# Attention with decay and a two-layer FFN on one core: reciprocals keyed earlier, two decay copies on ACT, buffers of the turned pairs relaid

## The chip, the cores and the metric

The kernel runs on 1 core of one Trainium2 chip. Times are device microseconds (us) of the whole program. A core has TensorE (PE, with its weight loads shown apart as PEld), VectorE (DVE), ScalarE (ACT), GpSimd (POOL) and SyncE (SP), each with a queue of its own that it works off in order. Matrix products go from SBUF into PSUM banks; DMAs are issued by SP, POOL or ACT.

## The reference

```python
def _attn_ref(q, k, v, f):                     # B, H, S, D = 8, 8, 576, 64
    scores = (1.0 / np.sqrt(D)) * np.matmul(q, k.transpose(0, 1, 3, 2))
    cum = np.cumsum(np.log(np.clip(f, 0.0001, 1.0)), axis=-1)
    decay = cum[:, :, :, None] - cum[:, :, None, :]
    scores = np.where(causal, -1000000000.0, scores + decay)   # causal: above the diagonal
    scores = scores - np.max(scores, axis=-1, keepdims=True)
    attn = np.exp(scores)
    attn = attn / (np.sum(attn, axis=-1, keepdims=True) + 1e-09)
    return np.matmul(attn, v)

x = attn_out.transpose(0, 2, 1, 3).reshape(B * S, H * D)       # 4608 x 512
h = x @ w_in                                                   # 512 -> 2048
g = np.maximum(h, 0.0) + alpha * np.minimum(h, 0.0)
return g @ w_out                                               # 2048 -> 512
```

All data are fp32.

## The kernel before

**Pairs.** The attention works on 32 pairs of heads, n = 4 b + p (batch b, pair p). `load_n` brings in what a pair needs, `attention` makes it up. For each pair: raw Q and K are loaded (L474, L475); from pair 4 on they are split into a high part on ACT (L537) and a low part on POOL (L538), and a score is three products; `Z` is the decay term of the four query tiles, with the causal mask added, and `Zt` that of the last 64 rows. DVE adds scores and decay and takes the row minimum (L744, L620), ACT takes the exponential and its row sum (L579), and the exponentials must then be transposed so that P·V can be multiplied.

**Two ways to transpose.** Pairs 0 to 9 transpose on PE, through PSUM. Pairs 10 to 31 (`NX = (10, 32)`) are "turned": the exponentials of a pair go into one buffer `bE`, DVE transposes it in 32 x 32 blocks into a buffer `bm` (L754), and sixteen DMAs of 96 KB move the blocks to their partitions in a buffer `bTT` (L764), which P·V reads. Of these sixteen, those with j % 8 in (2, 4, 6) are issued by POOL, the other ten by SP. There is one `bE`, two `bm` and one `bTT`: `bTT` is `wf[:, 0:3072]`, which is given to its ring in `o_cq` (L956), and `bE` and both `bm` are cut out of `big`, which `swap` (L963) gives to their rings when the P·V of pair 9 is done. The rings are `rE`, `rM` and `rTT`. Raw Q and K have a ring `rqk` of two buffers up to pair 10; from pair 11 on they use `rqk1`, whose one buffer also comes with `swap`.

**The decay of the turned pairs.** From pair NZ = 10 on, `Z` and `Zt` are made by DVE transposes of stored rows (L483, L485). Then, for each head, two copies (L501, L502) and four additions of the mask (L504) on POOL, and one addition for `Zt` (L529).

**Quotients.** From pair 6 on the row sums of two pairs are handled together: at the odd pair, `quotients` adds the epsilon on ACT (L670), takes the reciprocal on DVE (L671), transposes it on PE (L673), copies it on ACT (L674), stores it to DRAM from SP (L679), and `fetch` reads it back, spread over partitions, in three DMAs from SP for each of the two pairs (L686). The outputs of P·V, which ACT copies out of PSUM (L831), are multiplied with them (L844, for turned pairs on POOL) and split into high and low parts (L846, L848) for the FFN.

**FFN.** `ffn1` of a batch can start when its four pairs are done: 16 column blocks of 12 products each, the result evacuated by ACT and DVE (L925, L928, L930) and stored to DRAM (L932). `ffn2` follows after all of the attention, in tiles of seven products (Strassen's scheme in Winograd's form), every one as three products of high and low parts.

**What sets the order.** Nothing is ordered by hand. Every piece of work is an `op` with an engine, an estimated cost, a key, the ops it depends on and the buffers it takes. `Plan.run` is a list scheduler: again and again it takes, over all engines, the op that can start first by its estimates (the engine free, the inputs ready, a buffer free in each ring), and among those of one engine that can start at the same time the one with the smallest key. This fixes the order in each engine's queue before the kernel runs. Keys of a pair are built from `k0 = NS * n` with `NS = 10`, so 10 is one pair's distance. The moves of a pair have `k0 + 8`, `quotients` has `k0 + 11`, the loads have `kl = k0 - 16`, the decay `kc = k0 - 7`. On the chip an engine whose next instruction has to wait holds up all that are queued behind it.

Of the kernel before, what the change touches and what calls it, by code (L numbers as in the profile page):

```python
# [8 lines left out]
F32 = mybir.dt.float32  # L9
# [30 lines left out]
HURRY = 25  # L40
LAG = 1000
VK, TK = 0.65, 5
CONV0, CONV = 30, 2.2
# [160 lines left out]
def attention_moe(  # L204
# [21 lines left out]
    dram = ctx.enter_context(tc.tile_pool(name="dram", bufs=1, space=bass.MemoryType.DRAM))  # L226
    c8 = dram.tile([B * H, S], F32, name="c8")

    hd = dram.tile([NW, 2, 128, NT], F32, name="hd")
# [34 lines left out]
    qkt = [sp.tile([128, QW + S], F32, name=f"rqk{i}") for i in range(2)]  # L264
    rqk, rqk1 = Ring(Store(qkt)), Ring(Store([]))
    rZ = Ring(Store([(sp.tile([128, 2, ZW], F32, name=f"Z{i}"), sp.tile([128, S], F32, name=f"Zt{i}")) for i in range(2)]))
# [15 lines left out]
    cl = wf[0 : B * H, 0:S]  # L282
    G0 = 2 * NX[0]
    GN = B * H - G0
# [48 lines left out]
    def c_po(n):  # L333
        return 60 + 2.3 * n
# [48 lines left out]
    for i, (a0, a1) in enumerate(PC):  # L383
# [6 lines left out]
              -100, [o_sc[i]], [bcu, bft]) for i, (a0, a1) in enumerate(PC)]  # L390
    o_c8 = op("SP", 400, lambda: sy.dma_start(c8, ft()), -49, o_8, [bft], kb=147)
    o_id = op("POOL", 600, lambda: make_identity(nc, ident), -98)

# [67 lines left out]
    def load_n(n, held):  # L461
# [3 lines left out]
        kl, kc, bh = NS * n - 16, NS * n - 7, b * H + 2 * p  # L465
        bqk, bZ = Buf(rqk1 if n > NX[0] else rqk), Buf(rZ)
        q_, k_ = (lambda: bqk.t[:, 0:QW]), (lambda: bqk.t[:, QW : QW + S])
# [19 lines left out]
        for h in range(2):  # L487
            if spread:
                got = [zz]
            elif first:  # L490
                bz_ = Buf(rH)
                up = op("PE", 4 * c_mm(512), lambda h=h, bz_=bz_: mm(bz_.t, row()[:, h], ft()[:, 0:512], True, True), -60 + h, o_8 + [o_row], [bft, brow, bz_])
                got = [op("ACT", c_act(512), lambda h=h, bz_=bz_: ac.activation(Z()[:, h, 0:512], bz_.t, AF.Copy), -60, [up], [bz_, bZ])]
            else:
                got = [op("SP", 400, lambda h=h: sy.dma_start(Z()[:, h, 0:512], c8[bh + h : bh + h + 1, 0:512].broadcast_to([128, 512])),
                          kl + 1, [o_c8], [bZ], kb=256)]
            if n >= NX[0]:
                zp = lambda a, b, s, h=h: Z()[:, h, a:b].rearrange("p (k s c) -> p k s c", s=s, c=32)
                zd, zc, zb = (lambda zp=zp: zp(0, 512, 4)), (lambda zp=zp: zp(512, 896, 3)), (lambda zp=zp: zp(896, 1152, 2))
                za, tk = (lambda zp=zp: zp(1152, 1280, 1)), (lambda: tri.rearrange("p (k s c) -> p k s c", s=1, c=32))  # L500
                ms = [op("POOL", c_po(256) / 2, lambda zc=zc, zd=zd: po.tensor_copy(zc()[:, :, 0:2], zd()[:, :, 0:2]), kc + 0.1, got, [bZ]),  # L501
                      op("POOL", c_po(128) / 2, lambda zb=zb, zd=zd: po.tensor_copy(zb()[:, :, 0:1], zd()[:, :, 0:1]), kc + 0.2, got, [bZ])]  # L502
                for to, i in ((zc, 2), (zb, 1), (za, 0), (zd, 3)):
                    ms.append(op("POOL", c_po(128), lambda to=to, i=i, zd=zd: po.tensor_tensor(  # L504
                        to()[:, :, -1:], zd()[:, :, i : i + 1], tk(), ALU.add), kc + 0.1, got + [o_mask], [bZ]))
                rz.append(ms)
                continue
# [19 lines left out]
        else:  # L527
            tz = [op("SP", 400, lambda h=h: sy.dma_start(Zt()[64 * h : 64 * h + 64], c8[bh + h : bh + h + 1].broadcast_to([64, S])), kl + 1, [o_c8], [bZ], kb=147) for h in range(2)]
        rt = op("POOL", 260, lambda: po.tensor_tensor(Zt()[:, 512:576], Zt()[:, 512:576], tri2, ALU.add), kc + 0.3, tz + [o_mask], [bZ])  # L529
# [15 lines left out]
    def attention(n):  # L545
# [175 lines left out]
        def tile(h, i, st, bS, s, c0):  # L721
# [28 lines left out]
            if turned:  # L750
# [7 lines left out]
                if (h, i) == (1, 1):  # L758
                    e3.append(op("DVE", c_tr(768), lambda: turn(2, 288, 384), k0 + TK + 4, [be[g][m][1] for g in range(2) for m in (0, 1)], [bE, bm]))
                    got = []  # L760
                    for j in range(16):
                        a, k = j // 4, j % 4
                        q_, e_ = ((sy, "SP"), (po, "POOL"))[j % 8 in (2, 4, 6)]
                        got.append(op(e_, 600, lambda a=a, k=k, q_=q_: q_.dma_start(  # L764
# [119 lines left out]
        else:  # L884
            if mate:
                waiting.pop()
            quotients(k0 + 11 - hurry)
        later_x.append(rest)
# [66 lines left out]
    o_qc = [op("SP", 400, lambda a=a, c=c: sy.dma_start(c[32 * a : 32 * a + 32], c[0:32]), kc_ + 2, o_tc, kb=128) for a in range(1, 4) for c in (cq, cq2)]  # L955
    o_cq = op("-", 0, lambda: rTT.store.items.append(wf[:, 0:3072]) or rTT.store.free.append((plan.t, 0)), 0, o_tc + o_qc)  # L956

    def sides(h):
        for c, s0 in ((cq, 0), (cq2, 16)):
            po.tensor_copy(ct[64 * h : 64 * h + 64, s0 : s0 + c.shape[1], NX[0] :], c[64 * h : 64 * h + 64, :, h:GN:2])  # L960

    o_ct = [op("POOL", c_po(S) + 60, lambda h=h: sides(h), kc_ + 3, [o_cq]) for h in range(2)]
    def swap():  # L963
        for st, t in [(rE.store, big[:, 0:EW]), (rM.store, big[:, EW : EW + 3072]), (rM.store, big[:, EW + 3072 :]), (rqk1.store, qkt[0])]:
            st.free.append((plan.t, len(st.items)))
            st.items.append(t)
# [302 lines left out]
```

## Time and profile before

| | |
|---|---|
| median of 3 runs | 1046.42 us (1045.65 to 1049.57) |
| the profiled execution: time, span | 1045.14 us, 1043.3 us |
| granted TensorE clock, mean | 0.995 |
| PE busy | 1028.2 us, 99% of the span |
| DVE, ACT, POOL busy | 802.0, 631.2, 403.8 us |
| POOL, DMA issue of moves (L764) | 66.4 us in 132 |
| POOL, the copies L501 and L502 | 17.4 and 11.6 us, 44 of each |

The span goes from the first to the last instruction of the profiled execution; its time is 1.8 us longer. A group of the profile is told by its line in the kernel, its engine, its operation and "out<-in" by the program's names, with buffer numbers left out. "Idle before, releaser" is the time for which the engine stood still ahead of such instructions, and what ended it. SPq and POOLq are the DMA queues' own instructions, that is the issuing of DMAs.

### The profile page before, as it was taken

The page shows a single profiled execution, that of the slowest core. Times are in us where ns is not written, and L with a number is a line of the kernel's source. Part 1 is how long each engine was busy: PE and PEld are TensorE (multiplying, and loading weights), DVE is VectorE, ACT ScalarE, POOL GpSimd, SP SyncE. Part 2 cuts the span into 40 slices and gives each one's busy share as a digit, 9 for nine tenths or more (in the row PEclk, how much of TensorE's full clock was granted, in tenths as well). Part 3 has the DMA queues.
Part 4 walks back from the last instruction along what each step waited for, and adds up shares of the span by engine and source line. Part 5 has one row for each costly group of instructions (what it writes and reads, how often), then busy time and mean ns, then how long its engine had stood idle before and what let it go on. Part 6 is the DMA issues. An engine that isn't in the chain of part 4 may idle for free.

```text
span 1043.3 us, 22505 instructions
## 1 busy us (share of the span) xinstructions
PE 1028.2 (99%) x7994; PEld 899.7 (86%) x7994; DVE 802.0 (77%) x1702; ACT 631.2 (61%) x1462; POOL 403.8 (39%) x719
## 2 busy tenths in 40 slices
PE   9999999998999999999999999999999999999998
PEld 5888888787887787887888888899999999999998
DVE  5786885886776776767742987599898888989994
ACT  6779896675666666656552665655464545546551
POOL 6487674878887888886641000000000000000000
PEclk9999999998999999999999999999999999999999
DMA  5876754676888778886776666463434335344411
GB/s 173 236 224 209 231 171 131 195 218 180 254 236 224 233 225 229 245 242 183 213 207 194 213 222 203 166 201 121 140 123 140 122 122 161 117 129 139 124 62 41
DMA packets 125230, 187.74 MB, mean 180 GB/s; under 512 B 20967, under 2 KB 70622, under 8 KB 125118
## 3 DMA queue, kind: packets, MB, share of 16 engines
q1 hardware_dynamic: 120606, 173.13, 54.6%
q0 software_dynamic: 4224, 12.98, 4.8%
q8 instruction: 63, 1.03, 0.4%
q14 instruction: 49, 0.40, 0.1%
q10 hardware_dynamic: 288, 0.20, 0.1%
HBM read 102.80 MB, written 48.52 MB: 145 GB/s over the span
## 4 chain that ended last, share of the span: by engine, by line
PE 88%; POOL 4%; DMA 3%; DVE 2%; SPq 1%; issue 1%; ACT 1%; DVEq 0%; ACTq 0%; POOLq 0%
PE bank L362 84%; PE bank L592 2%; DMA rqk<-in_qk_dram 2%; SPq L764 1%; POOL Z L504 1%; PE bank L422 1%; POOL Ql L538 1%; POOL Kl L538 0%; DMA rd<-R 0%; PE bank L632 0%; DMA hd<-hs 0%; DVE big L744 0%; PE bank L456 0%; POOL xs L844 0%; POOL Z L510 0%
## 5 line engine op out<-in xcount | busy, mean ns | idle before, releaser
L362 PE MATMUL bank<-xx,wi 128*128 128x512 f32 x1728 | 418.2, 395 | 0.7 <-ACT eT L633 0.7
L362 PEld LDWEIGHTS bank<-xx,wi 128*128 128x128 f32 x1728 | 317.6, 188 | 74.1 <-issue 3.8
L579 ACT ACTIVATE big<-big,st 128x384 f32<-128x384 f32 (+4 forms) x268 | 156.1, 585 | 16.6 <-DVE st L744 15.1
L930 DVE SCALAR_TENSOR_TENSOR hs<-bank,sa,hs 128x512 f32<-128x512 f32 x96 | 71.7, 747 | 93.3 <-ACT hs L928 93.0
L362 PE MATMUL bank<-wot,xx 128*128 128x256 f32 x1008 | 123.9, 283 | 0.0
L362 PE MATMUL bank<-wi,xx 128*128 128x256 f32 x1008 | 123.9, 283 | 0.0
L362 PEld LDWEIGHTS bank<-wot,xx 128*128 128x128 f32 x1008 | 122.3, 192 | 0.0
L362 PEld LDWEIGHTS bank<-wi,xx 128*128 128x128 f32 x1008 | 122.3, 192 | 0.0
L744 DVE CUSTOM_DVE_ANT_0 big<-bank,Z 128x384 f32<-128x384 f32 (+3 forms) x211 | 92.9, 485 | 31.0 <-PE bank L362 22.9
L928 ACT ACTIVATE hs<-bank,ab 128x512 f32<-128x512 f32 x96 | 65.9, 686 | 82.5 <-PE bank L362 76.2
L754 DVE STREAM_TRANSPOSE big<-big 128x1152 f32<-128x1152 f32 (+1 forms) x66 | 79.3, 1221 | 13.6 <-ACT big L579 11.3
L764 POOL DMA_DIRECT2D wr<-big x132 | 66.4, 508 | 44.1 <-PE bank L632 24.7
L362 PE MATMUL bank<-wr,vr 128*64 128x128 f32 (+1 forms) x1232 | 68.3, 266 | 6.0 <-DMA wr<-big 4.2
L362 PEld LDWEIGHTS bank<-wr,vr 128*64 128x64 f32 x1232 | 60.1, 141 | 13.7 <-issue 6.9
L504 POOL TENSOR_TENSOR Z<-Z,tri 128x128 f32<-128x128 f32 x176 | 70.7, 428 | 0.0
L1153 ACT ACTIVATE xx<-gx 128x1024 fp32r<-128x1024 f32 x48 | 50.8, 1058 | 30.7 <-PE bank L362 15.1
L848 POOL TENSOR_TENSOR xx<-xs,xx 128x256 fp32r<-128x256 f32 x64 | 48.1, 764 | 49.4 <-ACT xx L846 49.0
L1156 DVE TENSOR_TENSOR xx<-gx,xx 128x1024 fp32r<-128x1024 f32 x48 | 58.5, 1218 | 7.9 <-ACT xx L1153 7.9
L362 PE MATMUL bank<-wi,gh 128*128 128x256 f32 x504 | 62.4, 283 | 0.0
L362 PE MATMUL bank<-wot,gh 128*128 128x256 f32 x504 | 62.4, 283 | 0.0
L362 PEld LDWEIGHTS bank<-wot,gh 128*128 128x128 f32 x504 | 61.4, 192 | 0.1
L362 PEld LDWEIGHTS bank<-wi,gh 128*128 128x128 f32 x504 | 61.3, 192 | 0.0
(157 smaller groups left out, 1749.4 us busy)
## 6 DMA issues: line engine op xcount, KB each, us to landing
hd<-hs SPq DMA_DIRECT2D x144, 256.0 KB
wx<-hd SPq DMA_DIRECT2D x47, 512.0 KB
wr<-big SPq DMA_DIRECT2D x220, 96.0 KB
rqk<-in_qk_dram SPq DMA_DIRECT2D x28, 512.0 KB
hr<-hd SPq DMA_DIRECT2D x25, 512.0 KB
wr<-big POOLq DMA_DIRECT2D x132, 96.0 KB, 3.7
vr<-in_vv_dram SPq DMA_DIRECT2D x32, 320.0 KB
wr<-in_w_in_dram SPq DMA_DIRECT2D x16, 512.0 KB
```

What stands on the lines that cost most here:

```text
L362: pe.matmul(o, lhsT, rhs, start=start, stop=stop)
L504: ms.append(op("POOL", c_po(128), lambda to=to, i=i, zd=zd: po.tensor_tensor(to()[:, :, -1:], zd()[:, :, i : i + 1], tk(), ALU.add), kc + ...
L579: ex = op("ACT", c_exp(w), lambda: ac.activation(at(bt.t), at(bt.t), AF.Exp, bias=lo()[:, col : col + 1], scale=-1.0, accum_out=su()[:, co ...
L592: pe.transpose(t[:, c : c + 128], src[:, 128 * j : 128 * j + 128], ident)
L744: ve.tensor_tensor_reduce(out=o if turned else blk(o), in0=blk(bS.t[:, c0 : c0 + w]), in1=in1(), scale=-0.125, scalar=3.0e38, op0=ALU.add, ...
L754: ve.transpose(part(bm.t), part(bE.t))
L764: got.append(op(e_, 600, lambda a=a, k=k, q_=q_: q_.dma_start(bTT.t[32 * k : 32 * k + 32, 768 * a : 768 * a + 768], bm.t[32 * a : 32 * a + ...
L848: xl = op("POOL", c_po(256), lambda r=r, t0=t0: po.tensor_tensor(bx.t[:, 1, t0 : t0 + 256], bxs[r].t[:, 0:256], bx.t[:, 0, t0 : t0 + 256]. ...
L928: cp = op("ACT", c_act(512), lambda bh=bh, bs=bs, fc=fc: ac.activation(bs.t, bh.t, AF.Relu, scale=ab[:, fc : fc + 1]), -1000, [last, o_sg] ...
L930: cp = op("DVE", c_dve(512), lambda bh=bh, bs=bs, fc=fc: ve.scalar_tensor_tensor(bs.t, bh.t, sa[:, fc : fc + 1], bs.t, ALU.mult, ALU.add), ...
L1153: his.append(op("ACT", c_acs(128 * GW * (j1 - j0)), lambda j0=j0, j1=j1, src=src, o_=o_: ac.activation(o_(0, j0, j1), src(), AF.Copy), key ...
L1156: rdy.append(op("DVE", c_dve(128 * GW * (j1 - j0)), lambda j0=j0, j1=j1, src=src, o_=o_: ve.tensor_tensor(o_(1, j0, j1), src(), o_(0, j0, ...
```

## The change

Four things are changed.

1. The key of `quotients` is lowered by 20 for turned pairs.
2. The two copies of the decay of a turned pair's head (L501, L502) are made by ACT instead of POOL, with the same keys and a cost estimate for ACT.
3. Buffers: `rqk1` is gone, so all raw Q and K share the ring `rqk` with its two buffers. `wf[:, 0:3072]` goes to `rM` (transposed blocks), and the last part of `big` goes to `rTT` (moved blocks). There are still one `bE`, two `bm` and one `bTT`.
4. A second copy of the decay rows in DRAM, `c8p`, whose columns are in the order of the turned pairs, is written by five DMAs from SP once `c8` is there. The loads of `Z` and `Zt` would read it for turned pairs below NZ; with `NX[0]` and NZ both 10 there is none. `PJ` names the three residues that were written out before, `G0` and `sides` name NZ where they named `NX[0]`, with the same values.

```diff
--- before.py
+++ after.py
@@ -39,6 +39,7 @@
 WC = 4
 HURRY = 25
 LAG = 1000
+PJ = (2, 4, 6)
 VK, TK = 0.65, 5
 CONV0, CONV = 30, 2.2
 NW = NF // 2
@@ -225,6 +226,7 @@
 
     dram = ctx.enter_context(tc.tile_pool(name="dram", bufs=1, space=bass.MemoryType.DRAM))
     c8 = dram.tile([B * H, S], F32, name="c8")
+    c8p = dram.tile([B * H, S], F32, name="c8p")
 
     hd = dram.tile([NW, 2, 128, NT], F32, name="hd")
     xt = dram.tile([NP, 128, 512], F32, name="xt")
@@ -262,7 +264,7 @@
 
     rQ = Ring(Store([split_set(i) for i in range(2)]))
     qkt = [sp.tile([128, QW + S], F32, name=f"rqk{i}") for i in range(2)]
-    rqk, rqk1 = Ring(Store(qkt)), Ring(Store([]))
+    rqk = Ring(Store(qkt))
     rZ = Ring(Store([(sp.tile([128, 2, ZW], F32, name=f"Z{i}"), sp.tile([128, S], F32, name=f"Zt{i}")) for i in range(2)]))
     vrt = sp.tile([128, 10, 2, D], F32, name="vr")
     rvr = Ring(Store([vrt[:, 5 * i : 5 * i + 5] for i in range(2)]))
@@ -280,7 +282,7 @@
     wf = wr.bitcast(F32)
     res = Ring(Store(cuts_of(1152, 2, 256) + [wf[:, 2560 + 256 * i : 2816 + 256 * i] for i in range(2)]))
     cl = wf[0 : B * H, 0:S]
-    G0 = 2 * NX[0]
+    G0 = 2 * NZ
     GN = B * H - G0
     cq = wf[:, 3072 : 3072 + 16 * GN].rearrange("p (s g) -> p s g", g=GN)
     rT4 = ring(sp, 2, [128, 128], F32, "eT4_")
@@ -389,6 +391,9 @@
     o_8 = [op("DVE", 150 + (a1 - a0) / 1.92, lambda a0=a0, a1=a1: ve.tensor_scalar_mul(ft()[:, a0:a1], cu()[:, a0:a1], -8.0),
               -100, [o_sc[i]], [bcu, bft]) for i, (a0, a1) in enumerate(PC)]
     o_c8 = op("SP", 400, lambda: sy.dma_start(c8, ft()), -49, o_8, [bft], kb=147)
+    o_c8p = [op("SP", 400, lambda k=k: sy.dma_start(c8p[:, 128 * k : 128 * k + 128].rearrange("p (s c) -> p s c", c=32),
+                                                    c8[:, 0:512].rearrange("p (s k c) -> p s k c", k=4, c=32)[:, :, k]), 6, [o_c8], kb=60) for k in range(4)]
+    o_c8p.append(op("SP", 400, lambda: sy.dma_start(c8p[:, 512:S], c8[:, 512:S]), 6, [o_c8], kb=16))
     o_id = op("POOL", 600, lambda: make_identity(nc, ident), -98)
 
     def make_mask():
@@ -463,7 +468,7 @@
         b, p = divmod(n, NP)
         first = n == 0
         kl, kc, bh = NS * n - 16, NS * n - 7, b * H + 2 * p
-        bqk, bZ = Buf(rqk1 if n > NX[0] else rqk), Buf(rZ)
+        bqk, bZ = Buf(rqk), Buf(rZ)
         q_, k_ = (lambda: bqk.t[:, 0:QW]), (lambda: bqk.t[:, QW : QW + S])
         kq = -99 if first else -59 if n == 1 else kl
         dq = [] if first else [o_scan]
@@ -492,14 +497,15 @@
                 up = op("PE", 4 * c_mm(512), lambda h=h, bz_=bz_: mm(bz_.t, row()[:, h], ft()[:, 0:512], True, True), -60 + h, o_8 + [o_row], [bft, brow, bz_])
                 got = [op("ACT", c_act(512), lambda h=h, bz_=bz_: ac.activation(Z()[:, h, 0:512], bz_.t, AF.Copy), -60, [up], [bz_, bZ])]
             else:
-                got = [op("SP", 400, lambda h=h: sy.dma_start(Z()[:, h, 0:512], c8[bh + h : bh + h + 1, 0:512].broadcast_to([128, 512])),
-                          kl + 1, [o_c8], [bZ], kb=256)]
+                c8_, o_ = (c8p, o_c8p) if n >= NX[0] else (c8, [o_c8])
+                got = [op("SP", 400, lambda h=h, c8_=c8_: sy.dma_start(Z()[:, h, 0:512], c8_[bh + h : bh + h + 1, 0:512].broadcast_to([128, 512])),
+                          kl + 1, o_, [bZ], kb=256)]
             if n >= NX[0]:
                 zp = lambda a, b, s, h=h: Z()[:, h, a:b].rearrange("p (k s c) -> p k s c", s=s, c=32)
                 zd, zc, zb = (lambda zp=zp: zp(0, 512, 4)), (lambda zp=zp: zp(512, 896, 3)), (lambda zp=zp: zp(896, 1152, 2))
                 za, tk = (lambda zp=zp: zp(1152, 1280, 1)), (lambda: tri.rearrange("p (k s c) -> p k s c", s=1, c=32))
-                ms = [op("POOL", c_po(256) / 2, lambda zc=zc, zd=zd: po.tensor_copy(zc()[:, :, 0:2], zd()[:, :, 0:2]), kc + 0.1, got, [bZ]),
-                      op("POOL", c_po(128) / 2, lambda zb=zb, zd=zd: po.tensor_copy(zb()[:, :, 0:1], zd()[:, :, 0:1]), kc + 0.2, got, [bZ])]
+                ms = [op("ACT", c_acs(256), lambda zc=zc, zd=zd: ac.activation(zc()[:, :, 0:2], zd()[:, :, 0:2], AF.Copy), kc + 0.1, got, [bZ]),
+                      op("ACT", c_acs(128), lambda zb=zb, zd=zd: ac.activation(zb()[:, :, 0:1], zd()[:, :, 0:1], AF.Copy), kc + 0.2, got, [bZ])]
                 for to, i in ((zc, 2), (zb, 1), (za, 0), (zd, 3)):
                     ms.append(op("POOL", c_po(128), lambda to=to, i=i, zd=zd: po.tensor_tensor(
                         to()[:, :, -1:], zd()[:, :, i : i + 1], tk(), ALU.add), kc + 0.1, got + [o_mask], [bZ]))
@@ -525,7 +531,7 @@
             tz = [op("ACT", c_act(a1 - a0), lambda b_=b_, a0=a0, a1=a1: ac.activation(Zt()[:, a0:a1], b_.t[:, 0 : a1 - a0], AF.Copy), -58, [up], [b_, bZ])
                   for b_, (a0, a1) in zip(bz2, cut)]
         else:
-            tz = [op("SP", 400, lambda h=h: sy.dma_start(Zt()[64 * h : 64 * h + 64], c8[bh + h : bh + h + 1].broadcast_to([64, S])), kl + 1, [o_c8], [bZ], kb=147) for h in range(2)]
+            tz = [op("SP", 400, lambda h=h, c8_=c8_: sy.dma_start(Zt()[64 * h : 64 * h + 64], c8_[bh + h : bh + h + 1].broadcast_to([64, S])), kl + 1, o_, [bZ], kb=147) for h in range(2)]
         rt = op("POOL", 260, lambda: po.tensor_tensor(Zt()[:, 512:576], Zt()[:, 512:576], tri2, ALU.add), kc + 0.3, tz + [o_mask], [bZ])
         if n < NN:
             held += [bqk]
@@ -760,7 +766,7 @@
                     got = []
                     for j in range(16):
                         a, k = j // 4, j % 4
-                        q_, e_ = ((sy, "SP"), (po, "POOL"))[j % 8 in (2, 4, 6)]
+                        q_, e_ = ((sy, "SP"), (po, "POOL"))[j % 8 in PJ]
                         got.append(op(e_, 600, lambda a=a, k=k, q_=q_: q_.dma_start(
                             bTT.t[32 * k : 32 * k + 32, 768 * a : 768 * a + 768], bm.t[32 * a : 32 * a + 32, 768 * k : 768 * k + 768]), k0 + 8 + j / 100, list(e3), [bm, bTT], kb=96))
                     e3[:] = [op("-", LAG, lambda: None, k0 + 8, got)]
@@ -884,7 +890,7 @@
         else:
             if mate:
                 waiting.pop()
-            quotients(k0 + 11 - hurry)
+            quotients(k0 + 11 - hurry - 20 * turned)
         later_x.append(rest)
         if n < NE - 1 or n == B * NP - 1:
             for f_ in later_x:
@@ -953,15 +959,15 @@
 
         o_tc.append(op("DVE", 340 + c_tr(S), spread_rows, kc_ + 1, o_cl + quick_ops + o_tc))
     o_qc = [op("SP", 400, lambda a=a, c=c: sy.dma_start(c[32 * a : 32 * a + 32], c[0:32]), kc_ + 2, o_tc, kb=128) for a in range(1, 4) for c in (cq, cq2)]
-    o_cq = op("-", 0, lambda: rTT.store.items.append(wf[:, 0:3072]) or rTT.store.free.append((plan.t, 0)), 0, o_tc + o_qc)
+    o_cq = op("-", 0, lambda: rM.store.free.append((plan.t, len(rM.store.items))) or rM.store.items.append(wf[:, 0:3072]), 0, o_tc + o_qc)
 
     def sides(h):
         for c, s0 in ((cq, 0), (cq2, 16)):
-            po.tensor_copy(ct[64 * h : 64 * h + 64, s0 : s0 + c.shape[1], NX[0] :], c[64 * h : 64 * h + 64, :, h:GN:2])
+            po.tensor_copy(ct[64 * h : 64 * h + 64, s0 : s0 + c.shape[1], NZ:], c[64 * h : 64 * h + 64, :, h:GN:2])
 
     o_ct = [op("POOL", c_po(S) + 60, lambda h=h: sides(h), kc_ + 3, [o_cq]) for h in range(2)]
     def swap():
-        for st, t in [(rE.store, big[:, 0:EW]), (rM.store, big[:, EW : EW + 3072]), (rM.store, big[:, EW + 3072 :]), (rqk1.store, qkt[0])]:
+        for st, t in [(rE.store, big[:, 0:EW]), (rM.store, big[:, EW : EW + 3072]), (rTT.store, big[:, EW + 3072 :])]:
             st.free.append((plan.t, len(st.items)))
             st.items.append(t)
 
```

## The prediction

> **What bounds the kernel now.** The page first: how busy the busiest engine is over the span.
>
> ```profile
> span 1043.3 us, 22505 instructions
> PE 1028.2 (99%) x7994; PEld 899.7 (86%) x7994; DVE 802.0 (77%) x1702; ACT 631.2 (61%) x1462; POOL 403.8 (39%) x719
> ```
>
> TensorE (PE) is idle for 1043.3 - 1028.2 = 15.1 us. The change adds and removes no matmul, so, slow clock apart, 15 us is about all that it can give. The view by stretches says where those 15 us lie. Columns: length, then busy us of PE, PEld, DVE, ACT, POOL, the granted clock, DMA share, GB/s. The turned pairs, which the change is about, lie between 180 and 560 us.
>
> ```profile
> 0.00:80.00 80.00, 76.71 (x645) 57.60 (x646) 57.84 (x175) 57.92 (x168) 52.01 (x98) 0.98 0.72 212
> 80.00:180.00 100.00, 100.00 (x837) 82.01 (x836) 71.20 (x158) 82.19 (x217) 61.46 (x85) 1.00 0.61 186
> 180.00:560.00 380.00, 371.80 (x2978) 300.70 (x2977) 269.21 (x641) 236.74 (x651) 286.43 (x533) 0.99 0.76 219
> 560.00:1043.30 483.30, 479.70 (x3540) 459.40 (x3538) 403.75 (x729) 254.39 (x429) 3.93 (x5) 1.00 0.45 142
> 241.00:248.00 7.00, 5.56 (x61) 5.27 (x61) 2.64 (x2) 1.78 (x5) 3.83 (x10) 0.51 0.47 144
> ```
>
> PE idles 3.3 us in the start, nothing from 80 to 180, 380 - 371.8 = 8.2 us among the turned pairs, and 3.6 us at the end, where only outputs are left. The change can reach the 8.2 us. The waits of PE between 160 and 560 us name them (total, times, longest):
>
> ```profile
> PE bank L362 <- DMA wr<-big: 4.2, 2, 3.6
> PE bank L362 <- DVE st L620: 1.4, 2, 0.7
> PE bank L362 <- ACT xs L831: 0.9, 1, 0.9
> PE bank L362 <- ACT eT L633: 0.7, 1, 0.7
> PE bank L673 <- DVE st L744: 0.4, 1, 0.4
> PE bank L362 <- DMA hd<-hs: 0.4, 1, 0.4
> ```
>
> One wait of 3.6 us is almost half of it. The timeline of PE shows what it really cost: the P·V products of one pair at full clock, and those after the wait, with the first instruction behind each.
>
> ```profile
> 228.00 1.75 PE L362 MATMUL bank<-wr,vr 128*64 128x128 f32 x28
> ...
> 230.91 0.33 PE L362 MATMUL bank<-Kh,Qh 64*128 64x128 f32 x2
> ...
> 242.44 3.26 PE L362 MATMUL bank<-wr,vr 128*64 128x128 f32 x28 [3.65 <-DMA wr<-big]
> ...
> 247.97 0.30 PE L632 MATMUL bank<-ident,big 128*64 128x128 f32 x1
> ```
>
> At full clock the products take 230.9 - 228.0 = 2.9 us; after the wait, at a clock of 0.51, 248.0 - 242.4 = 5.5 us. So this place costs 3.65 + 2.6 = 6.3 us, and the turned pairs hold 8.2 + 2.6 = 10.8 us in all. **That is the ceiling, 1.0%.** The bound for what can be told from no change is 0.5%, or 5.2 us.
>
> **Second raw Q, K buffer.** From pair 11 on all raw loads shared one buffer, so a load had to wait until the low parts of the pair before had been formed (SPq L474 <- POOL Kl). ACT runs in order and stands at the cast of Q until the load lands:
>
> ```profile
> SPq L474 <- POOL Kl L538: 5.7, 5, 2.5
> ```
>
> ```profile
> 332.53 0.74 ACT L537 ACTIVATE Qh<-rqk 128x640 fp32r<-128x640 f32 x1 [4.64 <-DMA rqk<-in_qk_dram]
> 333.18 0.25 ACT L633 ACTIVATE eT<-bank 64x128 f32<-64x128 f32 x1
> ...
> 396.81 0.74 ACT L537 ACTIVATE Qh<-rqk 128x640 fp32r<-128x640 f32 x1 [6.91 <-DMA rqk<-in_qk_dram]
> ...
> 399.98 0.37 ACT L831 ACTIVATE xs<-bank 128x256 f32<-128x256 f32 x1
> ```
>
> Behind the casts stand exactly the two ACT steps that PE waits for, L633 (0.7 us) and L831 (0.9 us). With two buffers the load is issued a pair earlier and both waits go: -1.6. What follows the second, the waits on DVE at L673 (0.4) and half of L620's (0.7), is ACT's lateness passed on: another -1.1. I take **-2.7**; bounds 0 (another step fills the same queue) and -3.8 (all six rows but the first: 1.4 + 0.9 + 0.7 + 0.4 + 0.4).
>
> **The 3.65 us place.** It is a wait for the sixteen moves into the transposed buffer (ten issued by SP, six by POOL):
>
> ```profile
> 214.92 7.75 SPq L764 DMA_DIRECT2D wr<-big  x10
> ...
> 232.05 8.01 SPq L764 DMA_DIRECT2D wr<-big  x10
> ...
> 242.46 0.29 SPq L679 DMA_DIRECT2D rd<-R  x1
> ...
> 248.06 7.76 SPq L764 DMA_DIRECT2D wr<-big  x10
> ...
> 255.87 0.60 SPq L686 DMA_DIRECT2D ri<-rd  x1
> ```
>
> There is one such buffer before and after the change; the relaying only says which memory it is and which two hold the transposes. So a pair's moves still wait for the P·V of the pair before (ended 230.9, moves from 232.05), and take 8.0 us to issue. The relaying by itself I cost at 0: the counts are the same, and the same transposes and moves read and write SBUF. Whether the order written by the planner again puts P·V too early for its moves, no row can say; the whole order of the turned pairs is worked out anew. I take half: **-3.1** (bounds 0 and -6.3).
>
> **Reciprocals earlier.** ACT's bias add, DVE's reciprocal, PE's turn (L673), ACT's copy, SP's store (L679) and the six fetches (L686) of two pairs all get a key 20 lower. Each small step now overtakes work on its engine; what matters is SP. The copy's store goes at 242.46, and the fetches at 255.87, behind the ten moves. Ordered by the new key they come between, ahead of the moves, and SP is in order: it holds the moves until the store has landed.
>
> ```profile
> SPq L686 <- DMA rd<-R: 13.6, 6, 3.5
> ```
>
> A wait is 13.6 / 6 = 2.3 us, and three fetches at 0.60 are 1.8 us: 4.1 us in front of the moves at worst, 0 if the planner sees a slot elsewhere. The cover is read from the landing of a last move, in the chain of waits:
>
> ```profile
> 239.49 2.52 DMA wr<-big
> ```
>
> The moves for the P·V at 228.0 were issued by 214.92 + 7.75 = 222.67 and, 2.5 us later, landed by 225.2: 2.8 us in hand. The likely delay is a part of that cover; I take **+1.5** in all over the 11 double pairs (bounds -0.4, L673's own wait gone, and 11 × 1.3 = +14).
>
> **Copies on ACT.** Rows of the same work on either engine:
>
> ```profile
> L501 POOL COPY Z<-Z 128x256 f32<-128x256 f32 x44 | 17.4, 394 | 3.3 <-DVE Z L483 3.3
> L502 POOL COPY Z<-Z 128x128 f32<-128x128 f32 x44 | 11.6, 291 | 0.0
> L846 ACT ACTIVATE xx<-xs 128x256 fp32r<-128x256 f32 x64 | 24.9, 411 | 13.2 <-POOL xs L844 8.0 <-DVE xs L844 3.3 <-PE bank L362 1.4
> L633 ACT ACTIVATE eT<-bank 64x128 f32<-64x128 f32 x22 | 5.7, 258 | 4.6 <-PE bank L632 4.6
> ```
>
> POOL, busy 286 of 380 us, loses 17.4 + 11.6 = 29.0 us, 1.3 us a pair; ACT, busy 237, gains 44 × (0.411 + 0.258) = 29.4 us and reaches 266, 70%. Neither is the bound. ACT's copies now stand in its queue before exponentials and evacuations and wait for DVE's transpose of the decay; if that is late, PE's waits on ACT come back. I take **0**, bounds -1.5 and +3.
>
> **The reordered decay in DRAM.** Five new copies after the store of c8. Nothing reads them, since turned pairs take their decay by the DVE transposes. They cost SP's time and DMA early on:
>
> ```profile
> 7.19 0.47 SPq L391 DMA_DIRECT2D c<-big  x1
> ...
> 10.43 1.35 SPq L528 DMA_DIRECT2D Zt<-c  x2
> 16.44 0.81 SPq L471 DMA_DIRECT2D rqk<-in_qk_dram  x2
> ```
>
> Five times 0.47 is 2.4 us, and SP has 16.44 - 11.78 = 4.7 us free before pair 2's load: **+0.5**, bounds 0 and +2.4 if they fall into a busier place. The Trainium skill, page "DMA: Bandwidth & Descriptors", Specifications, speaks against them: pieces under 512 bytes are read, modified and written, and four of the copies move 128-byte pieces. No row here shows such pieces from DRAM to DRAM; by that rule the upper bound would be the likelier.
>
> **The sum.** -2.7 - 3.1 + 1.5 + 0 + 0.5 = -3.8 us. On the profiled run's own 1045.1 us that is 1041.3; that run stands 1.3 us under the median of the three, 1046.4, so in the measure of medians **1042.6 us**.
>
> The clock bears on how much each left-over or new wait costs. A much shorter gap than 3.65 us also brought half clock:
>
> ```profile
> 64.00:67.00 3.00, 2.56 (x22) 2.05 (x20) 2.93 (x5) 0.91 (x2) 2.82 (x4) 1.00 0.85 192
> 67.00:70.40 3.40, 2.75 (x26) 2.75 (x28) 3.40 (x12) 2.18 (x6) 3.40 (x5) 0.50 0.90 315
> ```
>
> Here 0.44 + 0.65 = 1.1 us of idle was followed by 3.4 us at 0.50, a loss of some 1.4 us, while the waits of 0.9 us and less in the turned pairs lost none. So I price a new wait of 1 us or more at more than twice its length. The Trainium skill, page "TensorE: Matmul & The Clock Gate", Part 1, has the clock halve after an idle window of about 3.4 us; by that rule only a wait like the big one would be charged so, and new waits of 1 to 2 us would cost their length alone. The row at 67 us does not bear this out.
>
> **The rivals.**
> *All the stalls go.* Two raw buffers, an idler POOL and a planner with more room leave PE without gaps: -10.8 + 0.5, 1036.1 us. For it: 80 to 180 us has no idle at all. Against it: the waits are differences between planned and real times, and no estimate of the planner is changed.
> *Dealt anew.* The raw loads gain 2.7 us and the new order makes gaps of like size elsewhere, or the keys change little because DVE and ACT were free anyway: 1046 us. For it: the six rows are scattered, each with another releaser.
> *Slower: SP holds the moves.* Fetches ahead of the moves on SP, 4.1 us against a cover of 2.8 us: 1.3 us of PE at each of 11 double pairs, +14 in place of +1.5, with the other terms 1046.4 - 2.7 - 3.1 + 14 + 0.5 = 1055 us. It decides from the point where wait and fetches exceed the cover. For it: L686 waits up to 3.5 us. Against: the planner sees the store's landing, if too short, and can put FFN1 work ahead of P·V.
>
> **How the numbers follow.** Forecast 0.47; all gone 0.16; dealt anew 0.20; slower 0.17. The forecast's own spread is 1038 to 1046, of which a little over a third lies below 1041.2: 0.18 faster, 0.29 same. All gone is faster. Dealt anew is same but for 0.01 on either side. Slower: 0.15 beyond 1051.6, 0.02 same. Together 0.35, 0.49, 0.16. For 8 in 10 the range runs from the "all gone" case, 1036, to 1052, which takes in the nearer part of the slow case.
>
> **What would show it.** Right: ACT's casts at L537 no longer idle for 4 to 7 us on the raw load; the waits on L633 and L831 are gone from PE's list; no stretch among the turned pairs below clock 0.99; POOL 29 us less busy and ACT 29 us more. Wrong: PE idle in 180 to 560 us above 8 us; SP with fetches and waits on the store right ahead of the moves, and PE waiting for the moves in many pairs (slower); or a start that has lengthened by more than 2 us, seen in a later first P·V of a turned pair.

## The result and the profile after

The changed kernel takes 1034.97 us (median of 6 runs, 1033.04 to 1036.29) against 1044.23 us for the kernel before, whose three further runs beside it were lower than the first three (1040.69 to 1042.81). The ratio is 0.9903, 95% interval 0.9881 to 0.9924: faster by 1.0%, or some 10 us. (The two medians divided by one another give 0.9911, inside the interval.) The forecast was 0.9964 (1042.6 over 1046.4), a gain of 3.8 us, with a range that ended at 1036.0.

The page and the stretches of the kernel after, columns as before. Lines of the kernel after stand 2 to 6 further down than before (L362 is now L364, L744 is L750, L764 is L770).

```profile
span 1032.3 us, 22526 instructions
PE 1024.4 (99%) x7994; PEld 897.0 (87%) x7994; DVE 801.2 (78%) x1702; ACT 657.0 (64%) x1550; POOL 378.8 (37%) x631
```

```profile
0.00:80.00 80.00, 76.68 (x644) 57.53 (x645) 58.15 (x175) 57.92 (x167) 52.04 (x98) 0.98 0.75 214
80.00:180.00 100.00, 100.00 (x840) 82.25 (x839) 71.98 (x162) 85.91 (x230) 65.49 (x90) 1.00 0.65 202
180.00:560.00 380.00, 379.58 (x3028) 307.31 (x3027) 270.84 (x643) 262.52 (x734) 259.35 (x443) 1.00 0.77 221
```

The span is 11.0 us shorter. Of that, 7.8 us are idle time of PE between 180 and 560 us, now 0.4 instead of 8.2, and 2.6 us the half clock behind the long wait, which is gone (clock 1.00 instead of 0.99). The last 0.6 us I cannot place. The start is as it was. PE's waits after 80 us are these two; of the six rows of before, 8.0 us in all, only 0.2 us of the second is left:

```profile
PE bank L364 <- DVE st L626: 0.2, 1, 0.2
PE bank L364 <- issue: 0.2, 1, 0.2
```

So the case that the prediction called "all the stalls go" came true, at 0.16 of its chances. Why, the timelines of PE show. First the kernel before, from the P·V of pair 11 (228.00, shown above) to that of pair 12: these are all the FFN1 products (128x512) between the two.

```profile
231.85 3.00 PE L362 MATMUL bank<-xx,wi 128*128 128x512 f32 x12
...
236.21 1.67 PE L362 MATMUL bank<-xx,wi 128*128 128x512 f32 x6
```

And the same stretch after:

```profile
225.54 1.75 PE L364 MATMUL bank<-big,vr 128*64 128x128 f32 x28
...
229.35 1.66 PE L364 MATMUL bank<-xx,wi 128*128 128x512 f32 x6
...
230.88 3.00 PE L364 MATMUL bank<-xx,wi 128*128 128x512 f32 x12
...
235.23 3.06 PE L364 MATMUL bank<-xx,wi 128*128 128x512 f32 x12
...
238.15 1.63 PE L364 MATMUL bank<-xx,wi 128*128 128x512 f32 x6
...
240.51 1.75 PE L364 MATMUL bank<-big,vr 128*64 128x128 f32 x28
```

Before, PE had 18 FFN1 products to do while the moves of pair 12 were under way; after, 36. The moves are hardly sooner: SP had issued the last of them 12.1 us after the P·V of pair 11 had begun, after the change 11.1 us. P·V follows P·V by 14.4 us before and 15.0 after, but after, PE works through all of it. Before, it stood still because it had nothing else.

FFN1 has the largest keys of all work of this part (1e6 and up), so the planner puts it where PE has nothing else that can start as early: it is PE's filling work. Pair 11 is the last of batch 2 (pairs 8 to 11). By 228.0 us PE had done 384 FFN1 products, which is all of batches 0 and 1 (192 each), so FFN1 of batch 2 was what it had left. One block of it is two halves of 6 products: the first needs pairs 8 and 9, the second pairs 10 and 11; FFN1 of a batch can thus begin when two of its four pairs are done. The 18 are three first halves. For the second halves, the outputs of pairs 10 and 11 had to be multiplied with the reciprocals. In the changed kernel 12 of the 36 are the last block of batch 1, left over when the P·V of pair 11 began (372 products were done), and 24 are two whole blocks of batch 2.

SP's part of the chain of the reciprocals before: one store for pairs 10 and 11, three fetches for pair 10, three for pair 11.

```profile
212.48 0.29 SPq L679 DMA_DIRECT2D rd<-R  x1
...
223.35 1.75 SPq L686 DMA_DIRECT2D ri<-rd  x3
...
229.23 1.10 SPq L686 DMA_DIRECT2D ri<-rd  x2
...
231.48 0.48 SPq L686 DMA_DIRECT2D ri<-rd  x1
```

After:

```profile
206.76 0.30 SPq L685 DMA_DIRECT2D rd<-R  x1
...
210.18 1.76 SPq L692 DMA_DIRECT2D ri<-rd  x3
...
222.42 1.78 SPq L692 DMA_DIRECT2D ri<-rd  x3
```

The first fetches now come before the ten moves of pair 11, not behind them. What that does to POOL, which multiplies (L844, now L850) and splits (L848, now L854); before:

```profile
232.53 2.47 POOL L764 DMA_DIRECT2D wr<-big  x5
235.01 1.58 POOL L538 TENSOR_TENSOR Ql<-rqk,Qh 128x640 fp32r<-128x640 f32 x1
236.54 1.45 POOL L538 TENSOR_TENSOR Kl<-rqk,Kh 128x576 fp32r<-128x576 f32 x1
237.93 0.74 POOL L844 TENSOR_TENSOR xs<-xs,ri 128x256 f32<-128x256 f32 x1
...
241.62 0.72 POOL L848 TENSOR_TENSOR xx<-xs,xx 128x256 fp32r<-128x256 f32 x1
```

After:

```profile
230.37 1.59 POOL L850 TENSOR_TENSOR xs<-xs,ri 128x320 f32<-128x320 f32 x2
...
232.44 1.44 POOL L854 TENSOR_TENSOR xx<-xs,xx 128x256 fp32r<-128x256 f32 x2
```

Before, the multiplication of pair 11 came behind five moves and the split of the next pair, and the outputs were ready at 242.3, 14.3 us after their P·V had begun. After, they are ready at 233.9, 8.3 us after it.

### The profile page after: what moved, and what is told of

Same layout as the page of the kernel before. It is cut to its first block, busy times and chain, and to the rows that moved or that the text cites. A ratio compares the mean times of both kernels' runs of the same rounds, so it can differ in the third digit from the quotient of the medians.

```text
span 1032.3 us, 22526 instructions
## 1 busy us (share of the span) xinstructions
PE 1024.4 (99%) x7994; PEld 897.0 (87%) x7994; DVE 801.2 (78%) x1702; ACT 657.0 (64%) x1550; POOL 378.8 (37%) x631
## 4 chain that ended last, share of the span: by engine, by line
PE 96%; DVE 2%; POOL 1%; issue 0%; DMA 0%; ACT 0%; DVEq 0%
PE bank L364 92%; PE bank L598 2%; PE bank L427 1%; DMA wr<-in_w_in_dram 0%; PE bank L638 0%; DVE xs L850 0%; DVE wr L351 0%; POOL Z L516 0%; POOL wi L360 0%; DVE big L750 0%; PE bank L461 0%; PE bank L679 0%; DVE wr L355 0%; POOL Ql L544 0%; DVE wr L354 0%
## 5 line engine op out<-in xcount | busy, mean ns | idle before, releaser
L364 PE MATMUL bank<-xx,wi 128*128 128x512 f32 x1728 | 420.3, 397 | 0.0
L364 PEld LDWEIGHTS bank<-xx,wi 128*128 128x128 f32 x1728 | 316.4, 188 | 75.7 <-issue 8.3
L585 ACT ACTIVATE big<-big,st 128x384 f32<-128x384 f32 (+4 forms) x268 | 156.1, 584 | 14.3 <-DVE st L750 12.8
L364 PE MATMUL bank<-wi,xx 128*128 128x256 f32 x1008 | 123.9, 283 | 0.0
L364 PE MATMUL bank<-wot,xx 128*128 128x256 f32 x1008 | 123.9, 283 | 0.0
L364 PEld LDWEIGHTS bank<-wot,xx 128*128 128x128 f32 x1008 | 122.3, 192 | 0.0
L364 PEld LDWEIGHTS bank<-wi,xx 128*128 128x128 f32 x1008 | 122.3, 192 | 0.0
L750 DVE CUSTOM_DVE_ANT_0 big<-bank,Z 128x384 f32<-128x384 f32 (+3 forms) x211 | 92.7, 486 | 16.4 <-POOL Z L516 7.5
L364 PE MATMUL bank<-big,vr 128*64 128x128 f32 (+2 forms) x1752 | 96.9, 264 | 1.5 <-DVE st L626 1.3
L364 PEld LDWEIGHTS bank<-big,vr 128*64 128x64 f32 x1752 | 84.7, 139 | 10.9 <-issue 4.4
L854 POOL TENSOR_TENSOR xx<-xs,xx 128x256 fp32r<-128x256 f32 x64 | 48.4, 769 | 44.7 <-ACT xx L852 44.5
L364 PE MATMUL bank<-wi,gh 128*128 128x256 f32 x504 | 62.4, 283 | 0.0
L364 PE MATMUL bank<-wot,gh 128*128 128x256 f32 x504 | 62.4, 283 | 0.0
L364 PEld LDWEIGHTS bank<-wot,gh 128*128 128x128 f32 x504 | 61.4, 192 | 0.1
L364 PEld LDWEIGHTS bank<-wi,gh 128*128 128x128 f32 x504 | 61.3, 192 | 0.0
L364 PE MATMUL bank<-Kh,Qh 64*128 64x384 f32 (+3 forms) x280 | 59.1, 359 | 0.0
L931 ACT ACTIVATE hs<-bank,sg 128x512 f32<-128x512 f32 x48 | 33.0, 687 | 36.9 <-PE bank L364 32.1
```

Of the source, the lines that this page charges most:

```text
L364: pe.matmul(o, lhsT, rhs, start=start, stop=stop)
L585: ex = op("ACT", c_exp(w), lambda: ac.activation(at(bt.t), at(bt.t), AF.Exp, bias=lo()[:, col : col + 1], scale=-1.0, accum_out=su()[:, co ...
L750: ve.tensor_tensor_reduce(out=o if turned else blk(o), in0=blk(bS.t[:, c0 : c0 + w]), in1=in1(), scale=-0.125, scalar=3.0e38, op0=ALU.add, ...
L854: xl = op("POOL", c_po(256), lambda r=r, t0=t0: po.tensor_tensor(bx.t[:, 1, t0 : t0 + 256], bxs[r].t[:, 0:256], bx.t[:, 0, t0 : t0 + 256]. ...
L931: cp = op("ACT", c_act(512), lambda bh=bh, bs=bs, fc=fc: ac.activation(bs.t, bh.t, AF.Copy, scale=sg[:, fc : fc + 1]), -1000, [last, o_sg] ...
```

## The experiments

Every kernel was timed in five rounds beside the kernel before. Theories: **A**, the one raw buffer was what cost; **B**, each edit only has the planner deal a new order; **C**, the earlier key is what counts. After the first eight, **D** made C precise (the reciprocals come late, so FFN1 of the batch does, and PE runs out of filling work), against **E** (the moves themselves are late).

**One edit alone.** The kernel before with one part of the change each. Of an edit that stands in several places the line that says most is shown, and what is left out of a line is marked by dots.

```diff
-    rqk, rqk1 = Ring(Store(qkt)), Ring(Store([]))
+    rqk = Ring(Store(qkt))
```

> The kernel before with the second raw Q, K buffer for the turned pairs alone. Theory A (the one raw buffer holds ACT at its cast, and this is most of the 8.2 us of PE's idle time and of the half clock): 0.990 to 0.994 of before, PE idle between 180 and 560 us under 2 us, no waits of 4 to 7 us of the cast of Q on the raw load. Theory B (each edit only has the planner deal the order anew, and the gain is that of one lucky order): anything between 0.990 and 1.005, with the waits of the cast gone all the same. Theory C (the earlier key of the reciprocals is what counts): 0.998 to 1.000.

Measured 0.9947 (0.9931 to 0.9963). Half of the gain, which C had not expected; PE idles 3.2 us between 180 and 560, where A had expected under 2, as the long wait is still there:

```profile
232.13 1.66 PE L362 MATMUL bank<-xx,wi 128*128 128x512 f32 x6
...
233.65 3.00 PE L362 MATMUL bank<-xx,wi 128*128 128x512 f32 x12
...
242.52 3.26 PE L362 MATMUL bank<-wr,vr 128*64 128x128 f32 x28 [2.73 <-DMA wr<-big]
```

Again 18 products, then the wait.

```diff
-    o_cq = ... rTT.store.items.append(wf[:, 0:3072]) ...
+    o_cq = ... rM.store.items.append(wf[:, 0:3072]) ...
-        ... (rM.store, big[:, EW + 3072 :]) ...
+        ... (rTT.store, big[:, EW + 3072 :]) ...
```

> The kernel before with the transposed and the moved blocks of the turned pairs in each other's memory, as after, alone. Theory A: 1.000, within 0.002. Theory B: any side, up to 0.007 off. Theory C: 1.000.

Measured 1.0007 (0.9990 to 1.0024): nothing, as forecast.

```diff
-            quotients(k0 + 11 - hurry)
+            quotients(k0 + 11 - hurry - 20 * turned)
```

> The kernel before with the key of the quotients of turned pairs lowered by 20, alone. Theory A: 0.998 to 1.003, the waits on the raw load stay. Theory B: any side. Theory C: 0.990 to 0.994, and the wait of 3.65 us at the third turned pair's P V products gone.

Measured 0.9904 (0.9886 to 0.9923), the whole gain of the change from this one line. ACT still stood at its cast for the raw load:

```profile
L537 ACT ACTIVATE Qh<-rqk 128x640 fp32r<-128x640 f32 x28 | 20.6, 735 | 14.2 <-DMA rqk<-in_qk_dram 9.4 <-PE bank L362 4.8
```

9.4 us of those waits are left (14.9 in the kernel before), and PE idles for 0.1 us between 180 and 560. They cost PE no more than that once it has work in hand. Theory A, by which they were most of the loss, falls.

```diff
-                ms = [op("POOL", c_po(256) / 2, ... po.tensor_copy(zc()[:, :, 0:2], zd()[:, :, 0:2]) ...
+                ms = [op("ACT", c_acs(256), ... ac.activation(zc()[:, :, 0:2], zd()[:, :, 0:2], AF.Copy) ...
```

The copy of 128 columns goes with it.

> The kernel before with the two decay copies of a turned pair's head on ACT, alone. Theory A: 0.999 to 1.004, as ACT, which stands at the raw loads, gets 29 us more to do. Theory B: any side. Theory C: 1.000.

Measured 0.9951 (0.9934 to 0.9968), a gain that neither A nor C had expected, with a wait of 3.6 us for the moves of pair 12 still there.

**One edit taken back** from the changed kernel, each the reverse of the diffs above.

> The changed kernel with one raw Q, K buffer for pairs 11 to 31, as before. Theory A (the one raw buffer is what cost): 0.998 to 1.002 of before, with the waits of ACT's cast on the raw load back and PE idle of 6 to 9 us between 180 and 560 us. Theory B (only a lucky order): between 0.990 and 1.005. Theory C (the key): 0.990 to 0.994.

Measured 0.9903 (0.9880 to 0.9926), the same as the changed kernel, with 11.7 us of waits of the cast on the raw load; PE idles 1.6 us between 180 and 560, against 0.4:

```profile
L543 ACT ACTIVATE Qh<-rqk 128x640 fp32r<-128x640 f32 x28 | 20.6, 736 | 18.9 <-DMA rqk<-in_qk_dram 11.7 <-PE bank L364 6.5 <-issue 0.4
```

> The changed kernel with the old key of the quotients. Theory A: 0.988 to 0.993 of before, as the changed kernel. Theory B: between 0.990 and 1.005. Theory C: 0.998 to 1.002, with waits of PE at the turn of the reciprocals.

Measured 0.9935 (0.9912 to 0.9958). The wait at pair 12 is back, at 2.5 us, but there are 30 FFN1 products ahead of it, and most of the gain stays. Theory C had expected none to stay. Of the 30, 12 are left over from batch 1 and 18 are of batch 2, as many as before. And here the moves are late too: SP issues three of pair 12's, then the three fetches of pair 11 (230.11 to 233.49 us, with a store between), then the other seven, and the last is issued 14.1 us after the P·V of pair 11 had begun, against 11.1 in the changed kernel. At this place the old key costs in both ways, as theories D and E have it.

> The changed kernel with the two decay copies back on POOL. Theory A: 0.988 to 0.994 of before. Theory B: between 0.990 and 1.005. Theory C: 0.990 to 0.994.

Measured 0.9923 (0.9899 to 0.9947), which cannot be told from the changed kernel.

> The changed kernel with transposed and moved blocks in the memory they had before. Theories A and C: 0.990 of before, within 0.003. Theory B: between 0.990 and 1.005.

Measured 0.9891 (0.9866 to 0.9916), likewise.

**Which pairs.** The lower key at some double pairs only: `- 20 * (n == 11)`, `- 20 * (turned and n % 4 == 3)` and `- 20 * (turned and n % 4 == 1)` in place of `- 20 * turned`, and last `+ 10 * turned`.

> The kernel before with the lower key for the quotients of pairs 10 and 11 alone. Theory D (between the P V products of pairs 11 and 12 TensorE has no FFN1 work left, since FFN1 of batch 2 needs pairs 10 and 11, whose reciprocals come late; so it stands at the next P V until the moves have landed): the wait of 3.65 us and the half clock behind it gone, 0.993 to 0.996 of before, and 36 or more FFN1 products of 512 between these two P V in place of 18. Theory E (the moves themselves are late, and the key only deals a lucky order): the wait stays, or goes without more FFN1 products in between, 0.997 to 1.003.

Measured 0.9955 (0.9938 to 0.9972). The long wait is gone, with 42 products (12, 12, 6 and 12) in the gap, while the last move is issued 12.0 us after the P·V of pair 11 had begun, as late as in the kernel before (12.1). So here it is the filling work alone that takes the wait away. The last products and the P·V of pair 12:

```profile
243.90 3.01 PE L362 MATMUL bank<-xx,wi 128*128 128x512 f32 x12
246.84 1.75 PE L362 MATMUL bank<-wr,vr 128*64 128x128 f32 x28
```

> The kernel before with the lower key at pairs 11, 15, 19, 23, 27 and 31 alone, those that complete a batch. Theory D: most of what the lower key gives, 0.989 to 0.994 of before. Theory E: between 0.990 and 1.003, no better than the kernel with the key at the other pairs.

Measured 0.9928 (0.9911 to 0.9946), the long wait gone, with 42 products.

> The kernel before with the lower key at pairs 13, 17, 21, 25 and 29 alone, those that do not complete a batch. Theory D: the wait of 3.65 us stays, 0.997 to 1.002 of before. Theory E: between 0.990 and 1.003, no worse than the kernel with the key at the pairs that complete a batch.

Measured 0.9994 (0.9975 to 1.0013), with the long wait in place, at 2.5 us, behind 18 products. This pair of runs decides for D against E in the kernel before: the same number of double pairs, less one, and the key matters where a batch is completed and not elsewhere.

> The kernel before with the key of the quotients of turned pairs 10 higher. Theory D: FFN1 of each batch comes later still, TensorE waits more, 1.003 to 1.015 of before, with more waits on the moves. Theory E: 0.997 to 1.003.

Measured 0.9965 (0.9950 to 0.9980): theory D missed here. The long wait stayed, at 2.4 us, with 18 products ahead of it, but PE's later waits fell from 4.5 to 2.2 us instead of growing.

**Which part of the chain.** In `key_steps` the store and the fetches keep the old key (`key += 20 * turned` ahead of the store); in `key_sp` they alone get the lower one (`key -= 20 * turned` there, `quotients` as before).

> The kernel before with the key lowered by 20 for the steps of ACT, DVE and PE of the quotients alone; the store and the fetches of SP keep the old key. Theory D with the lateness in the fetches (in the kernel before the fetch for pair 11 is queued on SP until 232 us, long after the row sums are there): the wait at pair 12 stays, 0.996 to 1.001. With the lateness in the reciprocals: the wait is gone, 0.989 to 0.994.

Measured 0.9922 (0.9902 to 0.9943), the wait gone.

> The kernel before with the key lowered by 20 for SP's store and fetches alone; the reciprocals keep the old key. Theory D with the lateness in the fetches: the wait at pair 12 gone, 0.989 to 0.994. With the lateness in the reciprocals: the wait stays, 0.996 to 1.001.

Measured 0.9902 (0.9884 to 0.9920), the long wait gone; there are 24 products, and 1.1 us of waiting, for ACT, is left ahead of the P·V of pair 12. Here PE shows the real dependence openly, an FFN1 product that waits for the split outputs:

```profile
238.39 0.73 PE L362 MATMUL bank<-xx,wi 128*128 128x512 f32 x2 [0.55 <-POOL xx L849]
```

So no single step was late: moving either end of the chain brings the first fetches forward, to 212.8 and 216.5 us from 223.4, and that is enough.

**Controls.** The kernel before with one estimate of the planner changed by next to nothing, so that the same work is dealt in another order.

```diff
-LAG = 1000
+LAG = 1020
```

> A control: the kernel before with the planner's allowance for the landing of the moves 20 ns longer (1020 for 1000), nothing else. The work is the same, only the order of the turned pairs is worked out anew. Theory D (supply of FFN1 work after pair 11): the wait at P V of pair 12 stays with about 18 FFN1 products ahead of it; the later waits of PE, 4.6 us in all, may fall differently: 0.995 to 1.003 of before. If the later waits had causes in the raw buffer and in POOL alone: 1.000, within 0.002.

Measured 1.0009 (0.9997 to 1.0021). The second has `6 * 112 + 20` for `6 * 112` in `ns_v`.

> A second control: the kernel before with the planner's estimate of a turned pair's P V products 20 ns longer. Theory D: as the first control, the wait at pair 12 stays, 0.995 to 1.003 of before. If the later waits had causes in the raw buffer and in POOL alone: 1.000, within 0.002.

Measured 0.9973 (0.9955 to 0.9991). The third has 610 for 600 as the cost of a move.

> A third control: the kernel before with the planner's estimate of issuing a move 10 ns longer (610 for 600), nothing else. Theory D: the wait at P V of pair 12 stays with about 18 FFN1 products ahead of it. If a new order by itself is worth what the raw buffer alone and the copies alone gave: about 0.995 of before. If those two had a part of their own: 0.997 to 1.002, as the first two controls.

Measured 0.9953 (0.9935 to 0.9971). Its gain comes mostly from the later waits, of which 0.1 us is left of 4.5. The long one stays, behind 18 products, though the profile now names another releaser, and the P·V behind it takes 4.2 us where it took 5.5:

```profile
237.39 1.67 PE L362 MATMUL bank<-xx,wi 128*128 128x512 f32 x6
...
243.54 3.06 PE L362 MATMUL bank<-wr,vr 128*64 128x128 f32 x28 [3.57 <-DMA vr<-in_vv_dram]
```

A new order by itself was worth between +0.1% and -0.5% in these three. The raw buffer alone (0.9947) and the copies alone (0.9951) lie at the end of that spread; what of their gain is their own stays open.

**The unread copies.** The changed kernel without `c8p` and the five DMAs that write it.

> The changed kernel without the second copy of the decay rows in DRAM, which nothing reads. If its five DMAs cost at the start what the forecast put down, 0.5 us: 0.9898 of before against 0.9903, too little to be told apart. If they cost 2.4 us: 0.988 of before, and 2 us less in the first 80 us.

Measured 0.9904 (0.9886 to 0.9922): no cost that can be told. The changed kernel's SP shows why:

```profile
11.53 2.60 SPq L394 DMA_DIRECT2D c8p<-c  x4
14.17 0.61 SPq L396 DMA_DIRECT2D c8p<-c  x1
16.54 0.81 SPq L476 DMA_DIRECT2D rqk<-in_qk_dram  x2
```

They take 3.2 us of SP, where the prediction put 2.4, and fill the gap ahead of pair 2's load, which is issued at 16.54 instead of 16.44.

**All kernels together.** Counted up to the P·V of pair 12, the ten kernels in which the chain of pair 11 has no lower key (before, the three other single edits, the old key in the changed kernel, `key_middle`, `key_later` and the three controls) have each done exactly 18 products of batch 2, however their order was dealt, and PE waits there 2.4 to 3.9 us. In the ten in which all or a part of that chain has the lower key there are 24 or 42, second halves among them, and the wait is gone, but for the 1.1 us of `key_sp`. That the long wait hangs on the key of pair 11, and not on a lucky order, is thus shown; theory B is left for the later waits.

## Why the prediction was wrong

**The ceiling** was right: 10.8 us were to be had, and 10.4 of the 11.0 us gained are those.

**Reciprocals earlier (+1.5) failed, and the forecast with it.** Alone this edit gives 0.9904, some -10 us. The step looked only at what the moved chain costs on SP and never asked who waits for its result. The profile of before had two hints. POOL's multiplication stood idle for 26.8 us on the fetched reciprocals, and it does so for 12.1 us after:

```profile
L844 POOL TENSOR_TENSOR xs<-xs,ri 128x256 f32<-128x256 f32 (+1 forms) x44 | 35.2, 808 | 30.2 <-DMA ri<-rd 26.8 <-ACT Kh L537 1.7 <-ACT big L579 1.5
```

That is a hint and no price: with the copies alone on ACT these waits are 34.5 us, and the time falls all the same. And between two P·V there were 18 FFN1 products at one place and 30 or more at all others.

Of the 10 us, the 6.3 us of the long wait and its half clock are shown to come this way. The 4.5 us of later waits went too, but a control lost them with no edit of content, so for them the cause stays open.

The cost that I feared is there, and is covered: SP's waits for the store to land rose, and PE does not wait for the moves.

```profile
SPq L692 <- DMA rd<-R: 18.7, 10, 4.4
```

18.7 us in 10 times, from 13.6 in 6. With three fetches more in front of the moves, PE has 36 products to do meanwhile. At pair 12 it was even the old key that put fetches there: before, those of pair 11 were issued from 229.23 to 231.96 us, with the moves right behind at 232.05; after, at 222.42 us, before the P·V of pair 11.

**The 3.65 us place (-3.1)** was mis-sized and misread. The row named the moves as the releaser, and I took it for a question of the planner's timing that could go either way. It was a question of filling work, which the key settles: -6.3 us in the changed kernel, with a wait of 2.4 to 3.9 us still there wherever pair 11 has the old key or a later one.

**The second raw buffer (-2.7)** had the mechanism right as far as it went: ACT's stands of 4 to 7 us on the raw load are gone. But once FFN1 is supplied they cost nothing that the times can tell: taken back from the changed kernel, the ratio is 0.9903 again, with 1.2 us more idle time of PE. What the buffer gives alone, 0.9947, a control without content gives too (0.9953).

**Relaying (0) and unread copies (+0.5)** were right within what can be measured. **Copies on ACT (0)** were right by the edit taken back (0.9923, not to be told from 0.9903); alone they gave some -5 us, beyond the bound of -1.5, and whether that is their own stays open, as above. ACT's copies take 15.8 + 11.2 = 27.0 us, priced 29.4:

```profile
L507 ACT ACTIVATE Z<-Z 128x256 f32<-128x256 f32 x44 | 15.8, 406 | 2.9 <-DVE Z L488 2.9
L508 ACT ACTIVATE Z<-Z 128x128 f32<-128x128 f32 x44 | 11.2, 296 | 0.0
```

By the Trainium skill's rule that pieces under 512 bytes are read, modified and written ("DMA: Bandwidth & Descriptors", Specifications) the upper bound of 2.4 us had seemed the likelier for the unread copies. The time shows no such cost (0.9904 without them, 0.9903 with them); what became of the pieces themselves no run here shows.

**The chances.** What came true of "all the stalls go" is its time, and that by luck: the two raw buffers and the idler POOL that it rested on are not needed, as the kernel with the key alone has neither. I argued against it that the waits were differences between planned and real times. The controls bear that out for the later waits, not for the long one, which stayed in all three. Why PE had just three first halves ready there was not tried (in all kernels here no fourth block is begun at this place before a second half is done). All that I had listed as signs of being right came about (POOL 25.0 us less busy and ACT 25.8 us more, of the 29 named), so these signs did not tell the forecast from this rival.

## What to carry to other kernels

When the busiest engine waits, the releaser named is only the thing that ended the wait; count the filling work ahead of the wait and compare it with places where there was none, and follow what the filling work itself was waiting for. When an edit makes a short chain earlier, price what its result releases, not only the queues that it passes. And where a planner deals the order, time a change without content first: here such changes alone moved the time by up to 0.5%, so that a gain of that size from one edit proves little.

## What the runs showed of the clock

In the kernel with the key at pair 11 alone, a wait of 1.97 us was enough for half clock over the next 3.4 us; columns as before.

```profile
456.67 3.01 PE L362 MATMUL bank<-wr,vr 128*64 128x128 f32 x28 [1.97 <-DMA wr<-big]
```

```profile
453.00:456.70 3.70, 1.73 (x10) 1.14 (x9) 0.56 (x4) 2.15 (x5) 3.70 (x10) 1.00 0.69 180
456.70:460.10 3.40, 3.40 (x41) 3.40 (x43) 3.23 (x3) 0.00 (x0) 1.24 (x5) 0.54 0.81 225
```

So a wait of 2 us can cost nearly double: 3.4 us at 0.54 lose some 1.6 us. The prediction had put more than double on every new wait of 1 us or more, which is too much: in the same kernel a wait of 1.66 us, ahead of the P·V at 326.23 us, did not bring half clock, as the 28 products behind it took 1.75 us, like those at full clock. And the 1.1 us wait at 67 us, which had brought half clock in the kernel before, did not in the kernel with the key alone:

```profile
64.00:67.00 3.00, 1.90 (x19) 1.52 (x18) 2.97 (x7) 1.44 (x4) 2.23 (x4) 1.00 0.90 189
67.00:70.40 3.40, 3.40 (x61) 3.08 (x62) 3.36 (x11) 2.47 (x6) 3.40 (x5) 1.00 0.89 290
```

PE idles 1.1 us in these 6.4 us as before, and the clock stays at 1.00. The same gap can bring it or not.
